# A linear-attention chain with two MLPs on one core: the order of the opening stretch, where weight words are converted, and the width of the preparation stretches

## The chip, the core and the metric

The kernel runs on one core of one Trainium2 chip. The metric is device time in microseconds (us), from one execution of the whole program; less is better. The engines are named as in the profile: PE is TensorE's matmuls, PEld its weight loads, DVE is VectorE, ACT ScalarE, POOL GpSimd, and SP (SyncE) issues most of the DMAs. L12 is line 12 of the kernel.

## The reference

Three stages feed one another. The first is a delta-rule attention over 4 x 8 batch-heads, 768 time steps and head width 48:

```python
k_n = k / (np.linalg.norm(k, axis=-1, keepdims=True) + 1e-06)
for t in range(S):
    kt, vt, bt = (k_n[:, :, t], v[:, :, t], beta[:, :, t, None])
    y[:, :, t] = np.einsum('bhd,bhde->bhe', q[:, :, t], state)
    v_old = np.einsum('bhde,bhd->bhe', state, kt)
    state = state + bt[:, :, :, None] * np.einsum('bhd,bhe->bhde', kt, vt - v_old)
```

Its output, 3072 tokens of width 384, goes through a first MLP, `h = x @ w_in`, a leaky relu with a slope per column, `g @ w_out` (inner width 2048), and then through a second one, `(silu(x @ w_gate) * (x @ w_val)) @ w_out` (inner width 1536). The weights arrive as 64-bit floats, the rest as 32-bit floats.

## The kernel before

**Attention.** Time is cut into 24 chunks of 32 steps. Within a chunk the recurrence becomes a triangular system for each batch-head, and what is needed is the inverse of a unit triangular 32 x 32 matrix. Four chunks make a window, so a window has 128 such matrices (4 chunks x 32 batch-heads), one to a partition. `pre_T` transposes k and q on PE, `pre_G` makes the products of k with k (part 0, tile `GL`) and of k with q (part 1, tile `mt`), and the inverse is then made by one of two generators that are advanced a step at a time:

- `lanes` eliminates row by row: 31 steps of a multiply (L252) and a subtract (L260), the first 10 columns on VectorE and the others on GpSimd; with loads and transposes 37 steps. It uses no PE. Windows 2 to 5 use it.
- `lanes2` eliminates only two 16 x 16 blocks (L321, L323) and gets the rest from two products on PE: the first (L337, `out1`) for 16 matrices of each partition group at a time, `z` = 0 for chunks 0 and 1 of the window and `z` = 1 for chunks 2 and 3, then the second (L360) and a subtract (L369). Windows 0 and 1 use it.

`do_KS`, `do_QS`, `do_U`, `do_S`, `do_Y` and `do_XT` are then the recurrence of one chunk: small PE products, with a subtract, copies or adds on VectorE and ScalarE after each.

**Conversion.** No engine here takes 64-bit floats, so each weight slice (128 x 384) is turned into 32-bit words: one ScalarE operation (L514), three VectorE operations (L522, L524, L528), and then a split into a rounded part and a remainder: L535 on ScalarE, L536 on VectorE for odd slices and on GpSimd for even ones. The generator `conv` (`all_w1`) does this for the first MLP's 32 slices, 97 steps in all, three steps to a slice; `go(conv, 3)` is one slice.

**MLPs.** The first MLP takes two chunks (256 tokens) at a time: a block n has 16 units j. A unit is `H1` (nine PE matmuls, L595), two relus on ScalarE (L605, L606), a combination on VectorE (L608, tile `pn`), a split on ScalarE and GpSimd (L612, L613), and two and a half units later `O1` (nine matmuls, L624). So there are 12 blocks, of which block 0 runs beside the conversion. The second MLP (L682, L711) follows.

**Order.** The order of all work is written out by hand. `prelude` is a straight list: loads, window 0, chunks 0 and 1, and 16 steps of conversion in between. After it everything hangs on a table of events, each at a time counted in units, one unit being one `H1`: `at(time, function)`. Sorted, this gives the order on every engine; an engine then runs its instructions in that order. `base(c)` is the unit at which chunk c's recurrence begins (20 and 25.7 for chunks 4 and 5, 8(c-2) for the others), so window w is prepared in the 32 units from P = base(4w) - 32. PE's time ahead of the table is called the opening below.

Matmuls in 32-bit floats show two records each in the trace, so 64 small matmuls of the program are 128 records. `warm` issues matmuls on a constant.

Of the kernel before, what the change touches and what calls it, by code (L numbers as in the profile page):

```python
# [24 lines left out]
def kernel(  # L25
# [25 lines left out]
    nc = tc.nc  # L51
# [133 lines left out]
    class Lanes:  # L185
# [19 lines left out]
        def turn_X(self, i):  # L205
            r = slice(i * HC, i * HC + HC)
            nc.vector.transpose(TT_t[self.w].rearrange("p y i -> p i y")[:, r], self.X[:, r])

        def norm(self):
            self.s, self.r, self.n, self.a = (self.new("sm" + z, "sm" + z, [128, C]) for z in "srna")  # L210
            ss = free_view(self.L, 0, [[C + 1, C]])
            s0, r, a = self.s, self.r, self.a
            nc.scalar.activation(out=s0, in_=ss, func=AF.Sqrt)
            nc.vector.tensor_scalar(r, s0, 2e-6, 1e-12, op0=ALU.mult, op1=ALU.add)
            nc.vector.tensor_tensor(r, r, ss, ALU.add)
            nc.vector.reciprocal(r, r)
            nc.vector.tensor_tensor(a, r, self.bl, ALU.mult)
            nc.vector.tensor_copy(free_view(self.X, 0, [[C + 1, C]]), a)
# [78 lines left out]
    def lanes2(w, early=False):  # L297
# [29 lines left out]
        nc.gpsimd.memset(Dm[:, :, HC:C], 0.0)  # L327
        TT_t[w] = t.new("TT", "TT", [128, 32, C], 2)
        t.turn_X(1)
        yield  # L330
        G, TT = GL.pop(w), TT_t[w]
        ps = [bank(early and z == 1, "pi") for z in range(2)]

        def out1(z):
            for y in range(HC * z, HC * z + HC):
                for b in range(4):
                    nc.tensor.matmul(  # L337
                        ps[z][rows(b), (y % HC) * HC:(y % HC) * HC + HC],
                        G[rows(b), y, :],
                        TT[rows(b), y, HC:C],  # L340
                        start=True,
                        stop=True,
                        skip_group_check=True,
                    )

        N = HC * HC
        uv = t.new("tmp", "tmp", [128, 512])
        out1(0)
        nc.scalar.activation(out=uv[:, 0:N], in_=ps[0][:, 0:N], func=AF.Copy)
        out1(1)  # L350
        nc.scalar.activation(out=uv[:, N:2 * N], in_=ps[1][:, 0:N], func=AF.Copy)
        nc.vector.transpose(Dm.rearrange("p y s -> p s y")[:, 0:HC], t.X.rearrange("p i j -> p j i")[:, 0:HC])
        yield
        t.turn_X(0)
        yield
        for z in range(2):
# [14 lines left out]
            )  # L371
            yield

    LANES2 = 4 + HC - 1 + 5

    def rows(b):
        return slice(32 * b, 32 * b + 32)
# [77 lines left out]
                nc.scalar.activation(out=sv, in_=sp[a][:, 0:DM], func=AF.Copy)  # L455

    def do_Y(c):
        m, U, yp = m_t.pop(c), U_t.pop(c), y_ps.pop(c)
        for h in range(H):
            for b in range(4):  # L460
                nc.tensor.matmul(
# [313 lines left out]
    def prelude():  # L775
# [28 lines left out]
        load_nat(1, "k", nat)  # L804
        nc.sync.dma_start(out=alpha_r, in_=moe_alpha.rearrange("(j p) -> j p", p=128))
        load_k2(0)
        load_w1(4, 5, 6, 7)
        load_beta(1)
        go(conv, 3)
        for c in range(4):  # L810
            pre_G(c, (0,), early=c % 2 == 1)
        go(conv, 3)
        inv = lanes2(0, True)
        go(inv, 2)
        n = 0
        for b1 in range(2):
            for half in range(2):
# [13 lines left out]
            for half in range(2):  # L831
                pre_T(1, "k", b1, half, nat)
        load_nat(1, "q", nat)
        load_w1(8, 9, 10, 11)
        warm(12)
        go(inv, C)
        do_QS(0)
        do_U(0)
        pre_G(2, (1,), early=True)
        go(conv, 2)  # L840
        do_S(0)
        load_k2(1)
# [9 lines left out]
        do_U(1)
        go(conv, 2)
        for z in range(2):
            pre_T(1, "q", 0, z, nat)
        do_S(1)
        load_k2(2)
        load_w1(*range(20, 2 * J1))
        do_Y(1)
        go(conv, 2)  # L860
        for z in range(2):
            pre_T(1, "q", 1, z, nat)
# [11 lines left out]
    for w in range(1, NWIN):  # L874
        P = base(4 * w) - 32
        if w == 1:
            for z in range(4):
                at(0.6 + z, pre_G, 4 + z)
            l0, l1, n = 5, 18, LANES2
        else:  # L880
            at(P - 5, load_nat, w, "k", nat)
            at(P - 1, load_beta, w)
            for z in range(4):
                at(P + 1.2 + z, pre_T, w, "k", z // 2, z % 2, nat)
            at(P + 5, load_nat, w, "q", nat)
# [12 lines left out]
        for z in range(n):
# [97 lines left out]
```

## Time and profile before

| | us |
|---|---|
| median of 3 runs (lowest, highest) | 1206.99 (1203.62, 1210.70) |
| the profiled execution: its own time | 1208.26 |
| its span, first to last instruction | 1206.5 |
| opening, span's start to the first `H1` | 77.65 |
| block 0 of the first MLP (first `H1` to the next block's) | 92.85 |
| block 1 | 58.9 |
| PE busy / VectorE busy over the span | 1102.4 (91%) / 612.2 (51%) |

The shares over the whole span hide the stages: from about 740 us on, the second MLP keeps PE busy without a break, and nothing that is changed here lies there. What there is to read is the opening and the first MLP's blocks, each from its own stretch. Blocks are told by the start of their first `H1`.

### The profile page before, as it was taken

The numbers are of one execution on the slowest core, as the hardware profiler recorded it, in microseconds if no ns is written. First come the engines' busy times: TensorE is split into PE (matmuls) and PEld (weight loads), VectorE is DVE, ScalarE is ACT, GpSimd is POOL, SyncE is SP. The second block draws the span as 40 slices with busy tenths as digits, with TensorE's granted clock in tenths as the row PEclk, the third lists the DMA queues.
The fourth block names the chain that finished last, engine by engine and source line by source line (L and its number), as shares of the span: only waits on it lengthen the run. The fifth ranks groups of instructions, "written<-read, shape, count | busy, mean of one in ns | idle before, by whom it ended". The sixth has DMA issues, their size and how long they took to land.

```text
span 1206.5 us, 38212 instructions
## 1 busy us (share of the span) xinstructions
PE 1102.4 (91%) x16657; PEld 1063.2 (88%) x16657; DVE 612.2 (51%) x1283; ACT 444.8 (37%) x1160; POOL 313.6 (26%) x476
## 2 busy tenths in 40 slices
PE   6567779989998998999899998999999999999996
PEld 6556679889987998899799988999999999999995
DVE  5369952396369439736954346333333333333332
ACT  3145434425533543454344465222222222222221
POOL 4024222164237326423732356100000000000000
PEclk8588869989999999999999999999999999999998
DMA  9282003233323423342233145010101010101000
GB/s 216 81 280 42 2 3 81 55 94 96 80 68 82 117 58 82 86 101 69 56 89 83 31 145 151 1 40 1 40 1 40 1 40 1 40 1 40 8 13 20
DMA packets 140084, 76.50 MB, mean 63 GB/s; under 512 B 104000, under 2 KB 134624, under 8 KB 139916
## 3 DMA queue, kind: packets, MB, share of 16 engines
q1 hardware_dynamic: 139340, 73.45, 22.4%
q8 instruction: 130, 2.13, 0.7%
q0 software_dynamic: 576, 0.61, 0.2%
q14 instruction: 38, 0.31, 0.1%
HBM read 57.52 MB, written 16.52 MB: 61 GB/s over the span
## 4 chain that ended last, share of the span: by engine, by line
PE 58%; DVE 15%; issue 10%; POOL 4%; ACT 3%; DMA 1%; SPq 0%; POOLq 0%; DVEq 0%; ACTq 0%
PE gv L682 21%; PE o L711 10%; PE o L624 10%; PE h L595 10%; DVE pn L608 3%; DVE X L260 2%; DVE tmp L252 2%; PE pg L167 1%; POOL gh L613 1%; PE pt L148 1%; PE pk L396 1%; PE pst L440 1%; DVE wf L528 1%; DVE we L522 1%; PE py L396 1%
## 5 line engine op out<-in xcount | busy, mean ns | idle before, releaser
L682 PE MATMUL gv<-x2s,w 128*128 128x384 f32 x1728 | 316.9, 335 | 0.0
L682 PEld LDWEIGHTS gv<-x2s,w 128*128 128x128 f32 x1728 | 303.3, 188 | 0.0
L624 PE MATMUL o<-gh,w 128*128 128x256 f32 x1728 | 261.1, 294 | 29.2 <-ACT gh L612 13.8
L595 PE MATMUL h<-xh,w 128*128 128x256 f32 x1152 | 247.3, 291 | 17.1 <-ACT pn L606 14.7
L624 PEld LDWEIGHTS o<-gh,w 128*128 128x128 f32 x1728 | 224.8, 194 | 42.7 <-POOL gh L613 16.6
L613 POOL TENSOR_TENSOR gh<-pn,gh 128x256 fp32r<-128x256 f32 x192 | 150.2, 782 | 374.2 <-ACT gh L612 310.2
L595 PEld LDWEIGHTS h<-xh,w 128*128 128x128 f32 x1152 | 198.4, 197 | 21.9 <-ACT pn L606 16.7
L608 DVE SCALAR_TENSOR_TENSOR pn<-pn,nalpha 128x256 f32<-128x256 f32 x192 | 100.8, 525 | 178.9 <-ACT pn L606 175.9
L595 PE MATMUL h<-xl,w 128*128 128x256 f32 x576 | 166.6, 289 | 3.2 <-DVE xl L487 2.6
L711 PE MATMUL o<-w,us 128*128 128x384 f32 x864 | 165.3, 336 | 0.0
L612 ACT ACTIVATE gh<-pn 128x256 fp32r<-128x256 f32 x192 | 80.2, 418 | 224.3 <-DVE pn L608 224.3
L711 PEld LDWEIGHTS o<-w,us 128*128 128x128 f32 x864 | 151.1, 188 | 0.0
L694 DVE TENSOR_TENSOR sg<-sg,gv 128x384 f32<-128x384 f32 x96 | 53.2, 554 | 174.3 <-ACT sg L692 174.2
L595 PEld LDWEIGHTS h<-xl,w 128*128 128x128 f32 x576 | 113.6, 197 | 3.7 <-DVE xl L487 3.7
L697 ACT ACTIVATE us<-u 128x384 fp32r<-128x384 f32 x96 | 50.5, 526 | 165.0 <-DVE u L695 165.0
L667 POOL TENSOR_TENSOR x2s<-x2r,x2s 128x384 fp32r<-128x384 f32 x24 | 24.2, 1036 | 333.8 <-ACT x2s L666 333.8
L692 ACT ACTIVATE sg<-gv 128x384 f32<-128x384 f32 x96 | 47.1, 491 | 168.8 <-PE gv L682 168.8
L605 ACT ACTIVATE pn<-h 128x256 f32<-128x256 f32 x192 | 72.4, 377 | 99.7 <-PE h L595 97.1
L698 DVE TENSOR_TENSOR us<-u,us 128x384 fp32r<-128x384 f32 x96 | 53.7, 559 | 62.8 <-ACT us L697 62.8
L695 DVE TENSOR_TENSOR u<-sg,gv 128x384 f32<-128x384 f32 x96 | 53.2, 554 | 45.8 <-PE gv L682 45.6
L606 ACT ACTIVATE pn<-h 128x256 f32<-128x256 f32 x192 | 72.8, 379 | 0.0
L536 POOL TENSOR_TENSOR w<-wf,w 128x384 fp32r<-128x384 f32 x34 | 38.4, 1130 | 72.0 <-ACT w L535 70.8
(102 smaller groups left out, 1068.9 us busy)
## 6 DMA issues: line engine op xcount, KB each, us to landing
w<-in_moe_w_out_dram SPq DMA_DIRECT2D x28, 384.0 KB
w2d<-wf SPq DMA_DIRECT2D x36, 192.0 KB
wf<-w2d SPq DMA_DIRECT2D x36, 192.0 KB
w<-in_moe_w_in_dram SPq DMA_DIRECT2D x16, 384.0 KB
nat<-in_k_dram SPq DMA_DIRECT2D x24, 192.0 KB
k<-in_k_dram SPq DMA_DIRECT2D x96, 48.0 KB
x2d<-xs SPq DMA_DIRECT2D x12, 384.0 KB
w<-in_moe_w_gate_dram SPq DMA_DIRECT2D x12, 384.0 KB
```

The source lines that it names most:

```text
L595: nc.tensor.matmul(ps[:, 0:N1], w[:, a, kk * 128:kk * 128 + 128], x[b][:, kk, :], start=(i == 0), stop=(i == 3 * NK - 1),)
L605: nc.scalar.activation(out=pn[:, 1], in_=hv, func=AF.Relu, scale=-1.0)
L606: nc.scalar.activation(out=pn[:, 0], in_=hv, func=AF.Relu)
L608: nc.vector.scalar_tensor_tensor(out=g, in0=pn[:, 1], scalar=nalpha[:, j:j + 1], in1=pn[:, 0], op0=ALU.mult, op1=ALU.add)
L612: nc.scalar.activation(out=gh[:, 0], in_=g, func=AF.Copy)
L613: nc.gpsimd.tensor_tensor(gh[:, 1], g, gh[:, 0], ALU.subtract)
L624: nc.tensor.matmul(o[:, dm // 2, (dm % 2) * N1:(dm % 2) * N1 + N1], w[:, a, dm * 128:dm * 128 + 128], g[:, b], start=(j == 0 and i == 0 an ...
L682: nc.tensor.matmul(p[:, 0:N2], w2[j, z][:, a, kk * 128:kk * 128 + 128], x[:, b, kk], start=(i == 0), stop=(i == 3 * NK - 1),)
L694: nc.vector.tensor_tensor(sg, sg, ps[0], ALU.mult)
L695: nc.vector.tensor_tensor(u, sg, ps[1], ALU.mult)
L698: nc.vector.tensor_tensor(us[:, 1], u, us[:, 0], ALU.subtract)
L711: nc.tensor.matmul(o2_t[n][t][:, 0:DM], us[:, a, t * 128:t * 128 + 128], w[:, b, :], start=(j == 0 and i == 0), stop=(j == J2 - 1 and i == 2),
```

## The change

Line numbers in the changed file are 4 to 5 higher from L208 on, and 12 higher at the end. Four things are changed.

1. `lanes2` for window 0 makes the product pair of chunks 0 and 1 complete first; the second half's first product is issued behind it, and its second product and subtract at the end of the opening. The opening is written in another order around it, with fewer `warm` matmuls (4 and 6 instead of 8 and 12), and the k-q products of chunks 2 and 3 (`pre_G(2, (1,))`, `pre_G(3, (1,))`) move from the opening to units 0.6 and 1.6.
2. 41 steps of `conv` instead of 16 are issued in the opening, and 56 instead of 81 in units -0.5 to 13.5. Two more weight slices are loaded ahead of the q loads of window 1, and six instead of four behind them.
3. Window 1 uses `lanes` (37 steps, units 6.6 to 18.5) instead of `lanes2` (24 steps, units 5 to 18).
4. Windows 2 to 5: `lanes` runs from P+15 to P+31.5 instead of P+17.3 to P+31; q's loads move from P+5 to P+4.5, its transposes from P+9.2 to P+7.2, and `pre_G` from P+13.2 to P+11.2.

```diff
         TT_t[w] = t.new("TT", "TT", [128, 32, C], 2)
         t.turn_X(1)
-        yield
         G, TT = GL.pop(w), TT_t[w]
-        ps = [bank(early and z == 1, "pi") for z in range(2)]
+        ps = [None, None]
 
         def out1(z):
+            ps[z] = bank(early, "pi")
...
-        out1(0)
-        nc.scalar.activation(out=uv[:, 0:N], in_=ps[0][:, 0:N], func=AF.Copy)
-        out1(1)
-        nc.scalar.activation(out=uv[:, N:2 * N], in_=ps[1][:, 0:N], func=AF.Copy)
-        nc.vector.transpose(Dm.rearrange("p y s -> p s y")[:, 0:HC], t.X.rearrange("p i j -> p j i")[:, 0:HC])
-        yield
-        t.turn_X(0)
+        t.turn_Dm(Dm)
         yield
         for z in range(2):
+            out1(z)
+            nc.scalar.activation(out=uv[:, z * N:z * N + N], in_=ps[z][:, 0:N], func=AF.Copy)
+            if z == 0:
+                t.turn_X(0)
+            yield
...
-        load_w1(4, 5, 6, 7)
+        load_w1(*range(4, 10))
...
-        load_w1(8, 9, 10, 11)
-        warm(12)
-        go(inv, C)
+        load_w1(*range(10, 16))
+        warm(6)
+        go(inv, LANES2 - 13 - 4)
+        go(inv)
+        go(conv, 4)
+        go(inv)
+        go(conv, 2)
         do_QS(0)
         do_U(0)
-        pre_G(2, (1,), early=True)
-        go(conv, 2)
+        go(conv, 3)
         do_S(0)
...
-    CONV_DONE, CONV_END = 16, 14.0
+    CONV_DONE, CONV_END = 41, 14.0
...
+            for z in range(2):
+                at(0.6 + z, pre_G, 2 + z, (1,))
             for z in range(4):
-                at(0.6 + z, pre_G, 4 + z)
-            l0, l1, n = 5, 18, LANES2
+                at(2.6 + z, pre_G, 4 + z)
+            l0, l1, n = 6.6, 18.5, LANES
...
-            l0, l1, n = P + 17.3, P + 31, LANES
+            l0, l1, n = P + 15, P + 31.5, LANES
...
-                box["g"] = lanes2(w) if w == 1 else lanes(w, 10)
+                box["g"] = lanes(w, 10)
```

What stands on PE in the opening, from the `warm` matmuls to the second chunk, before (`pi` is the bank of the two products, `pg` of `pre_G`, `pu`, `pst`, `py`, `pk` and `px` of the recurrence):

```order
L742 MATMUL warm<-ident 96x96 x12
L337 MATMUL pi<-TT,GL 32x16 x128
L360 MATMUL pi<-tmp,Dm 32x16 x128
L422 MATMUL pu<-v,TT 32x48 x32
L167 MATMUL pg<-kqt 32x32 x32
L440 MATMUL pst<-U,k_105 64x48 x32
L461 MATMUL py<-U,mt 32x48 x32
L396 MATMUL pk<-St,kqt 32x48 x32
L396 MATMUL py<-St,kqt 32x48 x32
L167 MATMUL pg<-kqt 32x32 x32
L483 MATMUL px<-ident,ys 128x128 x3
L422 MATMUL pu<-v,TT 32x48 x32
```

And now:

```order
L746 MATMUL warm<-ident 96x96 x6
L342 MATMUL pi<-TT,GL 32x16 x64
L364 MATMUL pi<-tmp,Dm 32x16 x64
L342 MATMUL pi<-TT,GL 32x16 x64
L426 MATMUL pu<-v,TT 32x48 x32
L444 MATMUL pst<-U,k_105 64x48 x32
L400 MATMUL pk<-St,kqt 32x48 x32
L465 MATMUL py<-U,mt 32x48 x32
L400 MATMUL py<-St,kqt 32x48 x32
L426 MATMUL pu<-v,TT 32x48 x32
L487 MATMUL px<-ident,ys 128x128 x3
L465 MATMUL py<-U,mt 32x48 x32
```

One second product of 64 has gone to the end of the opening, where it stands ahead of window 1's last transposes and the first `H1`, and two `pg` groups of 32 have left the opening.

What stands on VectorE behind the subtract that completes the inverse of chunks 0 and 1, up to the copy of the first state, before (two subtracts, since both halves are done there):

```order
L369 TENSOR_TENSOR TT<-TT,pi 128x16x16 x2
L180 TENSOR_TENSOR mt<-pg,mask 128x256
L522 TENSOR_SCALAR we<-wf 128x384
L524 SCALAR_TENSOR_TENSOR wf<-wf,we 128x384
L536 TENSOR_TENSOR w<-wf,w 128x384
L453 COPY St<-pst 128x384
```

And now:

```order
L373 TENSOR_TENSOR TT<-TT,pi 128x16x16
L526 TENSOR_SCALAR we<-wf 128x384
L528 SCALAR_TENSOR_TENSOR wf<-wf,we 128x384
L540 TENSOR_TENSOR w<-wf,w 128x384
L532 SCALAR_TENSOR_TENSOR wf<-w_109,wf 128x384
L526 TENSOR_SCALAR we<-wf 128x384
L528 SCALAR_TENSOR_TENSOR wf<-wf,we 128x384
L532 SCALAR_TENSOR_TENSOR wf<-w_110,wf 128x384
L526 TENSOR_SCALAR we<-wf 128x384
L528 SCALAR_TENSOR_TENSOR wf<-wf,we 128x384
L540 TENSOR_TENSOR w<-wf,w 128x384
L532 SCALAR_TENSOR_TENSOR wf<-w_111,wf 128x384
```

Three slices of conversion (eleven instructions) now stand between that subtract and the state copy, where three instructions stood. Down to the first `pn` there are 13, 13, 12 and 7 of L526, L528, L532 and L540.

What stands on VectorE between two `pn` in the second half of block 0, before:

```order
L608 SCALAR_TENSOR_TENSOR pn<-pn,nalpha 128x256
L524 SCALAR_TENSOR_TENSOR wf<-wf,we 128x384
L536 TENSOR_TENSOR w<-wf,w 128x384
L528 SCALAR_TENSOR_TENSOR wf<-w_133,wf 128x384
L522 TENSOR_SCALAR we<-wf 128x384
L321 TENSOR_TENSOR tmp<-L,X 128x126
L323 TENSOR_TENSOR X<-X,tmp 128x2x9x7
L524 SCALAR_TENSOR_TENSOR wf<-wf,we 128x384
L528 SCALAR_TENSOR_TENSOR wf<-w_134,wf 128x384
L522 TENSOR_SCALAR we<-wf 128x384
L321 TENSOR_TENSOR tmp<-L,X 128x128
L323 TENSOR_TENSOR X<-X,tmp 128x2x8x8
```

And now:

```order
L612 SCALAR_TENSOR_TENSOR pn<-pn,nalpha 128x256
L257 TENSOR_TENSOR tmp<-L,X 128x220
L265 TENSOR_TENSOR X<-X,tmp 128x22x10
L528 SCALAR_TENSOR_TENSOR wf<-wf,we 128x384
L257 TENSOR_TENSOR tmp<-L,X 128x210
L265 TENSOR_TENSOR X<-X,tmp 128x21x10
L532 SCALAR_TENSOR_TENSOR wf<-w_136,wf 128x384
L257 TENSOR_TENSOR tmp<-L,X 128x200
L265 TENSOR_TENSOR X<-X,tmp 128x20x10
L526 TENSOR_SCALAR we<-wf 128x384
L528 SCALAR_TENSOR_TENSOR wf<-wf,we 128x384
L540 TENSOR_TENSOR w<-wf,w 128x384
```

Fewer conversions and three larger elimination steps stand between two `pn`. From the first `pn` of block 0 to that of block 1, VectorE now has 17 of L526, 17 of L528, 18 of L532 and 9 of L540, the first 30 of the 37 steps of `lanes`, 16 `pn`, and 14 operations of the attention (2 subtracts, 4 state adds, 6 `mt`, 2 `xl`).

## Rows read from the trace of the kernel before

**Rows 1.** Busy us and instructions by engine, clock, DMA: blocks 0 and 1.

```profile
core 0: us, PE busy (x) PEld busy (x) DVE busy (x) ACT busy (x) POOL busy (x), PEclk, DMA share, GB/s
77.65:170.50 92.85, 66.45 (x1428) 59.95 (x1428) 82.19 (x170) 44.27 (x113) 31.90 (x34) 0.81 0.21 58
170.50:229.40 58.90, 58.33 (x1421) 55.24 (x1414) 17.96 (x37) 26.87 (x77) 14.10 (x19) 0.92 0.26 61
```

**Rows 2.** Sum and mean of the same view over blocks 2, 4, 6 and 8.

```profile
sum 220.40, PE 195.82 PEld 183.45 DVE 186.01 ACT 78.84 POOL 119.88; mean PE 48.95 PEld 45.86 DVE 46.50 ACT 19.71 POOL 29.97
```

**Rows 3.** Sum and mean of the same view over blocks 3, 5 and 7.

```profile
sum 156.20, PE 154.56 PEld 147.45 DVE 65.86 ACT 83.15 POOL 47.11; mean PE 51.52 PEld 49.15 DVE 21.95 ACT 27.72 POOL 15.70
```

**Rows 4.** PE in the opening by time: start, us, what, xcount [idle before <-releaser].

```profile
40.18 1.84 PE L337 MATMUL pi<-TT,GL 32*32 32x16 f32 x123 [4.44 <-issue]
...
43.74 1.90 PE L360 MATMUL pi<-tmp,Dm 16*32 16x16 f32 x128 [1.67 <-issue]
47.20 1.84 PE L360 MATMUL pi<-tmp,Dm 16*32 16x16 f32 x124 [1.56 <-issue]
...
66.59 0.27 PE L422 MATMUL pu<-v,TT 32*32 32x48 f32 x4 [3.17 <-issue]
...
77.65 0.38 PE L595 MATMUL h<-xh,w 128*128 128x256 f32 x1 [0.58 <-ACT xh L486]
```

**Rows 5.** Busy time and DMA rate in one stretch of 2 us.

```profile
36.00:38.00 2.00, 0.00 (x0) 0.00 (x0) 0.00 (x0) 0.12 (x1) 0.00 (x0) 0.50 0.87 325
```

**Rows 6.** VectorE in block 0 by line: xcount | busy us, mean ns | idle before.

```profile
L524 DVE SCALAR_TENSOR_TENSOR wf<-wf,we 128x384 int32<-128x384 int32 x27 | 18.1, 672 | 1.1
L528 DVE SCALAR_TENSOR_TENSOR wf<-w,wf 128x384 int32<-128x384 int32 x27 | 18.0, 666 | 0.4
L522 DVE TENSOR_SCALAR we<-wf 128x384 int32<-128x384 int32 x26 | 13.7, 527 | 0.0
L536 DVE TENSOR_TENSOR w<-wf,w 128x384 fp32r<-128x384 f32 x14 | 9.1, 650 | 2.4 <-ACT w L535 2.4
L608 DVE SCALAR_TENSOR_TENSOR pn<-pn,nalpha 128x256 f32<-128x256 f32 x16 | 7.6, 476 | 0.0
...
L451 DVE TENSOR_TENSOR St<-pst,St 128x384 f32<-128x384 f32 x4 | 2.0, 547 | 0.0
L180 DVE TENSOR_TENSOR mt<-pg,mask 128x256 f32<-128x256 f32 x4 | 1.7, 420 | 1.4 <-ACT GL L177 1.3
...
L226 DVE TENSOR_SCALAR sms<-sms 128x32 f32<-128x32 f32 x1 | 0.2, 169 | 0.0
```

**Rows 7.** VectorE by time at the end of block 0.

```profile
173.68 0.48 DVE L608 SCALAR_TENSOR_TENSOR pn<-pn,nalpha 128x256 f32<-128x256 f32 x1 [7.30 <-ACT pn L606]
```

**Rows 8.** VectorE by line from 346 to 396 us, one whole run of `lanes`.

```profile
L252 DVE TENSOR_TENSOR tmp<-L,X 128x60 f32<-128x60 f32 (+29 forms) x31 | 12.2, 393 | 0.2
...
L524 DVE SCALAR_TENSOR_TENSOR wf<-wf,we 128x384 int32<-128x384 int32 x4 | 2.7, 684 | 0.0
...
L226 DVE TENSOR_SCALAR sms<-sms 128x32 f32<-128x32 f32 x1 | 0.2, 166 | 0.0
```

**Rows 9.** GpSimd by line over the same stretch.

```profile
L252 POOL TENSOR_TENSOR tmg<-L,X 128x21 f32<-128x21 f32 (+10 forms) x21 | 8.6, 408 | 0.9
L260 POOL TENSOR_TENSOR X<-X,tmg 128x21 f32<-128x21 f32 (+10 forms) x21 | 7.8, 371 | 1.6
```

**Rows 10.** GpSimd by line in block 0.

```profile
L536 POOL TENSOR_TENSOR w<-wf,w 128x384 fp32r<-128x384 f32 x14 | 15.6, 1112 | 20.4 <-ACT w L535 20.1
L613 POOL TENSOR_TENSOR gh<-pn,gh 128x256 fp32r<-128x256 f32 x16 | 13.3, 830 | 49.3 <-issue 33.5 <-ACT gh L612 9.7 <-DMA w<-in_moe_w_in_dram 3.1
```

**Rows 11.** PE by time in block 4, its longest wait.

```profile
372.36 0.38 PE L624 MATMUL o<-gh,w 128*128 128x256 f32 x1 [2.82 <-ACT gh L612]
```

**Rows 12.** PE by time in block 1: the second products of window 1.

```profile
174.68 1.91 PE L360 MATMUL pi<-tmp,Dm 16*32 16x16 f32 x128
...
179.58 1.26 PE L360 MATMUL pi<-tmp,Dm 16*32 16x16 f32 x128
```

**Rows 13.** Block 3 by time: q's loads on SP, and its first transpose on PE.

```profile
298.32 3.79 SPq L100 DMA_DIRECT2D nat<-in_q_dram  x4
...
315.58 0.60 PE L148 MATMUL pt<-ident,nat 128*128 128x128 f32 x4
```

More of the change, by code (lines that the diff above doesn't have):

```diff
@@ L207, in turn_X, with turn_Dm @@
             nc.vector.transpose(TT_t[self.w].rearrange("p y i -> p i y")[:, r], self.X[:, r])
+        def turn_Dm(self, Dm):
+            nc.vector.transpose(
+                Dm.rearrange("p y s -> p s y")[:, 0:HC], self.X.rearrange("p i j -> p j i")[:, 0:HC]
+            )
         def norm(self):
@@ L372, in lanes2 @@
             yield
-    LANES2 = 4 + HC - 1 + 5
+    LANES2 = 4 + HC - 1 + 6
     def rows(b):
@@ L457, in do_Y @@
     def do_Y(c):
-        m, U, yp = m_t.pop(c), U_t.pop(c), y_ps.pop(c)
+        m, U, yp = m_t.pop(c), U_t[c], y_ps.pop(c)
         for h in range(H):
@@ L813, in prelude @@
         inv = lanes2(0, True)
-        go(inv, 2)
+        go(inv, 3)
         n = 0
@@ L843, in prelude @@
         load_v(2)
-        load_w1(*range(12, 20))
+        load_w1(*range(16, 24))
+        go(conv, 3)
+        do_KS(1)
+        go(conv, 3)
         do_Y(0)
-        do_KS(1)
-        go(conv, 2)
         do_QS(1)
-        pre_G(3, (1,), early=True)
+        do_U(1)
+        go(conv, 3)
         do_XT(0)
         go(conv, 2)
[L852 to L855, printed above, removed]
+        do_Y(1)
+        go(conv, 3)
         do_S(1)
         load_k2(2)
[L858 to L862, printed above, removed]
-        do_XT(1)
-        go(conv, 2)
+        load_w1(*range(24, 2 * J1))
+        go(conv, 3)
+        do_XT(1)
+        go(conv, 3)
+        go(inv)
+        go(conv, 3)
+        go(inv)
+        for z in range(4):
+            pre_T(1, "q", z // 2, z % 2, nat)
+        go(conv, 3)
     def base(c):
         return {4: 20, 5: 25.7}.get(c, 8 * (c - 2))
-    CONV_DONE, CONV_END = 16, 14.0
+    CONV_DONE, CONV_END = 41, 14.0
     CONV_N = 3 * 2 * J1 + 1 - CONV_DONE
@@ L884 @@
                 at(P + 1.2 + z, pre_T, w, "k", z // 2, z % 2, nat)
-            at(P + 5, load_nat, w, "q", nat)
+            at(P + 4.5, load_nat, w, "q", nat)
             for z in range(4):
-                at(P + 9.2 + z, pre_T, w, "q", z // 2, z % 2, nat)
+                at(P + 7.2 + z, pre_T, w, "q", z // 2, z % 2, nat)
             for z in range(4):
-                at(P + 13.2 + z, pre_G, 4 * w + z)
-            l0, l1, n = P + 17.3, P + 31, LANES
+                at(P + 11.2 + z, pre_G, 4 * w + z)
+            l0, l1, n = P + 15, P + 31.5, LANES
         box = {}
```

2 lines of the change are left out of this document (1 added, 1 removed).

## The prediction

> **What bounds the kernel now.** I read stretch by stretch, since the shares of the whole span mix stages with different limits. From about 740 us PE works without a break and nothing changed lies there, so the time has to come out of the opening, of blocks 0 and 1, and of the blocks that prepare a window.
>
> The windows of blocks 0 and 1 come first [rows 1]. In block 0 VectorE is busy 82.19 of 92.85 us while PE has 66.45, so VectorE is the bound and it idles 10.66 us. Of this, 7.30 lie at one place at the block's end: VectorE, whose next instruction is a `pn`, waits for ScalarE's relu, which follows an `H1` [rows 7]; ahead of that `H1` PE stands in `lanes2`'s products of window 1. Block 1 is the opposite: PE 58.33 of 58.90, VectorE 17.96, and a mean granted clock of 0.92 of 2.4 GHz, so it spent some of its time at 1.2 GHz.
>
> The later blocks alternate. The even ones, with `lanes` in them, last 220.40/4 = 55.1 us with PE busy 48.95, so PE idles 24.58 us over the four [rows 2]; their VectorE is busy 46.5. The odd ones last 156.20/3 = 52.07 with PE at 51.52 [rows 3]. In the even blocks, then, PE waits, and its longest wait in block 4 is an `O1` for `gh`, 2.82 us [rows 11]: a chain from VectorE's `pn` through ScalarE that stands in VectorE's queue behind elimination steps.
>
> The opening, by PE's order of time [rows 4], is a third kind. PE starts again at 40.18, 43.74 and 47.20, each time for 1.84 to 1.90 us of 123 to 128 records, after waits of 1.56 to 1.67 that the trace puts to nothing ("issue"). So a set of 128 records costs some 3.5 us whatever it computes, half of it waiting for instructions. The wait of 4.44 comes just behind a stretch in which the weight loads move 325 GB/s [rows 5].
>
> The skill's "Runtime: NRT & Kernel Launch", section "Instruction fetch mechanics", says that instructions come in blocks of 256 and that crossing a block is mostly hidden. The trace disagrees here: 128 matmul records with as many weight loads are followed by 1.6 us of waiting [rows 4]. By the page, removing 128 records would save only their some 1.9 us of execution.
>
> **The change part by part.** The sum is made against the profiled execution's own 1208.26 us (a span of 1206.5 and 1.8 around it); the median of the runs shown is 1.27 lower.
>
> *Opening, -0.7.* Two `pg` groups, 64 products or 128 records, leave: one period, 43.74 - 40.18 = 3.55 us less. `lanes2` has as many products as before. Two more weight slices (2 x 384 KB, 1.2 us each at 325 GB/s [rows 5]) go ahead of the q loads and prolong the burst in which the 4.44 wait lies: +2.4. The first `H1` waits 0.58 for the `xh` of chunk 1 [rows 4]; the half product now put between hides this and about as much again: -1.0. Along the recurrence some eight hand-offs from PE to VectorE or ScalarE and back now may find conversion in front. VectorE's load down to the first `pn`, at block 0's durations [rows 6], is 13 x .527 + 13 x .672 + 12 x .666 + 7 x .650 = 28.1 us, which fits into the 33.9 us from 43.74 to 77.65, but not loosely. I take two hand-offs that meet half a slice (some .75 us each): +1.5. Together -0.65. Bounds: all eight meeting a whole slice's VectorE operations (about 1.9) would be +15; at the other end `H1` comes 9 earlier, if supply waits go with the burst (4.44 and 3.17) beside the removed period, less the 2.4.
>
> *Block 0, -10.4.* VectorE is the bound, so I count its work from the first `pn` to the next block's. Conversion, 17 x .527 + 17 x .672 + 18 x .666 + 9 x .650 = 38.2; 16 `pn`, 7.6; 14 attention operations, 8 x .547 + 6 x .420 = 6.9 [rows 6]. A whole `lanes` costs VectorE 34.2, the sum of the 17 groups in which its lines show from 346 to 396 us [rows 8]. Of its 37 steps 30 fall here, 27.7 by count; the last ones are the shortest, so I take 30 (bounds 27.7 and 34.2). Sum 82.7. Block 0's 27 groups add up to 91.4 where the busy union is 82.19, since neighbours overlap: a factor of .90, hence 74.4. For idle time I take 8, between 10.66 - 7.30 = 3.4 (the one wait gone, with the products that made it) and 55.1 - 46.5 = 8.6 (even blocks). Block 0 is then 82.4, not 92.85. The two `pg` groups that arrive cost PE at most 3.55, hidden while PE has 66.45; if that cover goes they are on the path. L524 takes 684 ns beside `lanes` against 672 without [rows 6, 8], so no surcharge on conversion. Bounds: -17 (27.7 for `lanes`, 3.4 idle: 72.4 + 3.4) and +3 (34.2, no overlap factor, 8.6 idle: 86.9 + 8.6).
>
> *Block 1, -4.6.* The second products of window 1 on PE, 1.91 + 1.26 [rows 12], vanish: -3.2. What the clock cost is .08 x 58.9 = 4.7; with a block 0 in which PE idles less, I give back a third, -1.4. `lanes`' last seven steps, some 4 us, hide under VectorE's 41 us of idle time. Bounds -3.2 and -7.9.
>
> *Blocks 2, 4, 6, 8, -12.3.* `lanes` spread over 16.5 units instead of 13.7. What elimination adds to VectorE is the even less the odd blocks' busy time, 46.50 - 21.95 = 24.55: over 13.7 units 1.79 us each, beside 21.95/16 = 1.37 of other work [rows 2, 3]. So in the stretch VectorE has 3.16 per unit against PE's 48.95/16 = 3.06: slightly over. After: 24.55/16.5 + 1.37 = 2.86, under PE. A small change turns the inequality, but waits from order stay, so I take half of the 24.58 PE idle. Bounds 0 and -24.6. q's loads move half a unit earlier and its transposes two, so the transposes come 1.5 units or some 4.9 us nearer to their loads. Before, the four loads ran from 298.32 for 3.79 us and the first transpose came at 315.58 [rows 13]: of the 13.5 us between, 8.6 are left, and the move costs nothing. GpSimd's part, 16.4 [rows 9], has more room, too.
>
> Sum: -0.7 - 10.4 - 4.6 - 12.3 = -28.0, so 1180.3 on the profiled time and **1179** on the median.
>
> **The rivals.** *A, the opening is held up.* VectorE and ScalarE take their queues in order, and three slices of conversion now stand between the completed inverse and the first state's copy. If six of eight hand-offs meet a slice's 1.9 us, `H1` comes 10 us later than forecast: 1189. For it: 28.1 us in 33.9. Against: PE's own supply takes 3.5 us per 128 records, in which VectorE gets through more than a slice.
>
> *B, the wider stretch gives nothing.* PE's waits in the even blocks are waits for order (`pn` behind any elimination step, then `gh` [rows 11]) and not load; then they last 16.5 units at a lower price each, and -12.3 falls away: 1191. For it: 46.5 of 55.1 is no full VectorE.
>
> *C, everything loosens.* The even blocks lose all idle time (-12.3 more) and the burst's waits vanish from the opening (-3.3 more): 1163.
>
> *D, slower: VectorE and GpSimd exclude each other in block 0.* Into the block that VectorE bounds come 16.4 us of `lanes` on GpSimd [rows 9], beside 13.3 of `gh` and nine conversions of 1.112, 10.0 [rows 10]. If none of these 39.7 us runs beside VectorE, block 0 is 74.4 + 39.7 + 8 = 122.1, +29.3 instead of -10.4: 1219. It decides from 28 of the 39.7 us on. Against: in the even blocks VectorE's 46.5 and GpSimd's 30.0 lie within 55.1 us [rows 2], so at least 21.4 overlap as recorded, though a blocked instruction may count as busy.
>
> In the skill, "SBUF — State Buffer", section "Who interferes with whom", says that a VectorE instruction with two inputs in SBUF and a GpSimd one that reads SBUF lock each other out for the whole instruction. By that rule D would hold for most pairs here; L524's 684 against 672 [rows 6, 8] does not show it.
>
> **How the numbers follow.** Forecast .52 (its own range 1169 to 1189), A .16, B .14, C .09, D .09. The likeliest gives 1179. The range leaves out D and the far half of C, and reaches from 1162 to 1202, where A and B together (1201) end. A difference of 0.5%, 6 us, is about what can be told from none (the runs spread over 7), so "same" is 1201 to 1213. Faster .86: the forecast, A and B but for .05 in which they fall together, and C; same .09: that .05 and half of D where the lock-out is partial; slower .05.
>
> **What would show it.** Right: the first `H1` at about 77 us; block 0 near 82 with VectorE busy near 74 and no single wait of 7 us; no `lanes2` products in block 1 and its length near 54; even blocks near 52 with shorter waits of PE for `gh`. Wrong: the first `H1` after 85, with VectorE or ScalarE named before PE's starts (A); even blocks still at 55 (B) or at 49 (C); GpSimd and VectorE instructions of block 0 longer than 1112, 830 and 672 ns, and the block over 93 (D). The forecast as a whole fails if the opening grows by as much as block 0 shrinks, because conversion has then only moved from one bound stretch to another.

## The result and the profile after

The changed kernel takes 1177.82 us (median of 4 runs, 1175.76 to 1178.39), the kernel before 1206.28 (4 runs): a ratio of 0.9757, 95% interval 0.9725 to 0.9789. The forecast was 1179 within 1162 to 1202. The profiled execution took 1177.41 us against 1208.26, 30.85 less. The sum came out, in part by luck: the terms of the stretches are off by 2.5 to 7.5 us each, in both directions.

| | before | after | change | forecast |
|---|---|---|---|---|
| opening, to the first `H1` | 77.65 | 69.41 | -8.2 | -0.7 |
| block 0 | 92.85 | 85.0 | -7.9 | -10.4 |
| block 1 | 58.9 | 58.6 | -0.3 | -4.6 |
| blocks 2, 4, 6, 8 | 220.4 | 199.0 | -21.4 | -12.3 |
| blocks 3, 5, 7 | 156.2 | 162.3 | +6.1 | 0 |
| all behind | | | +0.8 | 0 |

Blocks 0 and 1 by windows, after (columns as in [rows 1]: stretch, length, then busy us of PE, PEld, DVE, ACT, POOL, granted clock, DMA share, GB/s):

```profile
69.42:154.41 84.99, 64.15 (x1304) 58.01 (x1301) 72.34 (x152) 37.40 (x100) 42.41 (x66) 0.78 0.18 46
154.41:213.00 58.59, 56.28 (x1222) 53.01 (x1222) 26.57 (x64) 27.50 (x81) 16.61 (x26) 0.95 0.28 66
```

VectorE has 72.34 us in block 0 (forecast 74.4), but idles 12.65, not 8. In block 1 PE is busy 2.05 us less (forecast 4.6, of products and of clock), and yet the block is no shorter: PE now idles 2.31 us in it, 1.97 of them at its end, where the first `H1` of block 2 waits for the attention's output `xh`. Sum and mean of the even blocks 2 to 8 and, in the second fence, of the odd ones 3 to 7, against [rows 2] and [rows 3]:

```profile
sum 199.00, PE 183.68 PEld 173.63 DVE 179.40 ACT 79.62 POOL 119.76; mean PE 45.92 PEld 43.41 DVE 44.85 ACT 19.90 POOL 29.94
```

```profile
sum 162.30, PE 158.39 PEld 150.60 DVE 70.47 ACT 82.55 POOL 46.53; mean PE 52.80 PEld 50.20 DVE 23.49 ACT 27.52 POOL 15.51
```

PE's idle time in the even blocks fell from 24.6 to 15.3 us, and its busy time by 12.1: the last of a window's four `pre_G` groups, which stood in them, has moved into the odd block before (for window 2, into block 1), and the granted clock in them rose, from 0.97 to 1.00 in block 4. The odd blocks got 1.28 us of PE work each, and 0.75 of idle time.

PE in the opening by time, after (columns as in [rows 4]):

```profile
31.78 1.90 PE L342 MATMUL pi<-TT,GL 32*32 32x16 f32 x128 [6.08 <-DVE TT L207]
34.23 0.50 PE L364 MATMUL pi<-tmp,Dm 16*32 16x16 f32 x21 [0.55 <-issue]
35.30 1.62 PE L364 MATMUL pi<-tmp,Dm 16*32 16x16 f32 x106 [0.56 <-issue]
...
41.49 1.62 PE L342 MATMUL pi<-TT,GL 32*32 32x16 f32 x106 [4.29 <-issue]
...
45.60 1.17 PE L426 MATMUL pu<-v,TT 32*32 32x48 f32 x43 [2.02 <-issue]
...
69.41 0.37 PE L599 MATMUL h<-xh,w 128*128 128x256 f32 x1
```

The 4.29 us wait beside the weight loads is the 4.44 of [rows 4], no longer for the two more slices (in the nine kernels with PE's order as changed and 16 or 41 conversion steps it is 3.75 to 5.39, in the mean 4.4); the first `H1` waits for nothing; and the first product of the inverse starts at 31.78, where it started at 33.78. From that start to the first `H1`, PE's waits without a named releaser ("issue") add up to 9.9 us, and to 16.2 before; those for VectorE or ScalarE to 3.3, and 1.4 before. So the opening's gain lies mostly in the waits that the trace puts to nothing.

What VectorE waited for in block 0, after (engine, waiting line, releaser: us in all, times, longest):

```profile
DVE mt L180 <- ACT GL L177: 4.6, 4, 2.9
DVE w L540 <- ACT w L539: 3.3, 4, 1.9
DVE pn L612 <- ACT pn L610: 1.4, 2, 1.0
...
```

The wait of 7.30 for a `pn` [rows 7] is gone. The largest is now `mt`: its multiply stands in VectorE's queue for products that PE has not yet made, and everything else on VectorE stands behind it.

How VectorE sets the end of block 0 shows on ScalarE and PE there, by time:

```profile
153.56 0.42 ACT L616 ACTIVATE gh<-pn 128x256 fp32r<-128x256 f32 x1 [3.87 <-DVE pn L612]
153.88 0.47 ACT L490 ACTIVATE xh<-px 128x384 fp32r<-128x384 f32 x1
154.40 0.58 PE L599 MATMUL h<-xh,w 128*128 128x256 f32 x1 [2.73 <-ACT xh L490]
```

ScalarE waits 3.87 us for a `pn`, which VectorE makes behind elimination steps; the copy of `xh` stands behind that in ScalarE's queue, and block 1's first `H1` waits for `xh`.

### The profile page after: what moved, and what is told of

It reads as the page before. It is cut to its first block, busy times and chain, and to the rows that moved or that the text cites. A ratio compares the mean times of both kernels' runs of the same rounds, so it can differ in the third digit from the quotient of the medians.

```text
span 1175.7 us, 37218 instructions
## 1 busy us (share of the span) xinstructions
PE 1087.1 (92%) x16125; PEld 1049.6 (89%) x16125; DVE 621.9 (53%) x1313; ACT 444.4 (38%) x1158; POOL 330.4 (28%) x517
## 4 chain that ended last, share of the span: by engine, by line
PE 60%; DVE 19%; issue 13%; ACT 3%; POOL 2%; DMA 1%; POOLq 0%; DVEq 0%; SPq 0%; ACTq 0%
PE gv L686 21%; PE o L715 10%; PE o L628 10%; PE h L599 10%; DVE tmp L257 4%; DVE pn L612 3%; DVE X L265 2%; PE pg L167 2%; DVE wf L532 1%; PE pt L148 1%; PE pst L444 1%; PE py L465 1%; DVE wf L528 1%; PE pk L400 1%; POOL w L540 1%
## 5 line engine op out<-in xcount | busy, mean ns | idle before, releaser
L628 PE MATMUL o<-gh,w 128*128 128x256 f32 x1728 | 258.2, 293 | 22.8 <-POOL gh L617 9.6
L599 PE MATMUL h<-xh,w 128*128 128x256 f32 x1152 | 243.6, 288 | 12.7 <-ACT pn L610 6.7
L628 PEld LDWEIGHTS o<-gh,w 128*128 128x128 f32 x1728 | 223.1, 193 | 35.6 <-POOL gh L617 13.7
L599 PEld LDWEIGHTS h<-xh,w 128*128 128x128 f32 x1152 | 195.8, 194 | 15.7 <-ACT pn L610 7.3
L698 DVE TENSOR_TENSOR sg<-sg,gv 128x384 f32<-128x384 f32 x96 | 53.2, 554 | 175.9 <-ACT sg L696 175.9
L702 DVE TENSOR_TENSOR us<-u,us 128x384 fp32r<-128x384 f32 x96 | 53.7, 559 | 62.8 <-ACT us L701 62.8
L699 DVE TENSOR_TENSOR u<-sg,gv 128x384 f32<-128x384 f32 x96 | 53.2, 554 | 45.7 <-PE gv L686 45.5
L257 DVE TENSOR_TENSOR tmp<-L,X 128x31 f32<-128x31 f32 (+29 forms) x155 | 65.7, 424 | 1.4
```

Of the source, the lines that this page charges most:

```text
L257: eng.tensor_tensor(w, t.L[:, i + 1:C, i:i + 1].to_broadcast([128, n, m]), t.X[:, i:i + 1, c0:c0 + m].to_broadcast([128, n, m]), ALU.mult,)
L599: nc.tensor.matmul(ps[:, 0:N1], w[:, a, kk * 128:kk * 128 + 128], x[b][:, kk, :], start=(i == 0), stop=(i == 3 * NK - 1),)
L628: nc.tensor.matmul(o[:, dm // 2, (dm % 2) * N1:(dm % 2) * N1 + N1], w[:, a, dm * 128:dm * 128 + 128], g[:, b], start=(j == 0 and i == 0 an ...
L698: nc.vector.tensor_tensor(sg, sg, ps[0], ALU.mult)
L702: nc.vector.tensor_tensor(us[:, 1], u, us[:, 0], ALU.subtract)
```

## The experiments

Twelve kernels, each timed in three rounds beside the kernel before. "First `H1`" and the lengths are from each one's profiled execution. "As changed" is the changed kernel.

| | us | ratio, interval | first `H1` | block 0 | block 1 | blocks 4, 6, 8, mean |
|---|---|---|---|---|---|---|
| as changed | 1177.8 | 0.976 (.973, .979) | 69.4 | 85.0 | 58.6 | 49.1 |
| 16 conversion steps | 1194.7 | 0.989 (.987, .992) | 71.8 | 98.0 | 58.5 | 49.0 |
| products back | 1180.9 | 0.978 (.976, .981) | 74.8 | 81.2 | 58.1 | 49.1 |
| `lanes2` for window 1 | 1178.1 | 0.976 (.974, .978) | 72.0 | 71.3 | 70.0 | 49.0 |
| before, part 4 alone | 1195.4 | 0.990 (.987, .993) | 77.6 | 93.2 | 61.3 | 49.0 |
| narrow | 1191.3 | 0.985 (.983, .987) | 72.0 | 83.1 | 57.2 | 53.2 |
| early and narrow | 1187.7 | 0.982 (.980, .984) | 73.3 | 82.2 | 58.4 | 52.0 |
| column 24, window 1 | 1178.5 | 0.974 (.973, .976) | 71.5 | 80.5 | 62.8 | 49.1 |
| 47 conversion steps | 1175.9 | 0.973 (.970, .975) | 74.7 | 79.5 | 58.1 | 49.0 |
| halves together | 1179.8 | 0.977 (.974, .980) | 74.9 | 81.2 | 58.4 | 49.1 |
| 18 units | 1168.6 | 0.967 (.962, .971) | 68.8 | 82.5 | 57.9 | 47.0 |
| column 7 | 1186.8 | 0.983 (.979, .986) | 70.7 | 82.3 | 58.4 | 50.8 |
| 18 units, column 16, chunks 4 and 5 earlier | 1157.8 | 0.958 (.956, .961) | 70.1 | 84.1 | 57.0 | 45.6 |

**16 conversion steps.** Some of the `go(conv, n)` of the opening are cut or left out:

```diff
-    CONV_DONE, CONV_END = 41, 14.0
+    CONV_DONE, CONV_END = 16, 14.0
```

> The changed kernel with only 16 steps of conversion in the opening, as before, and 81 in units -0.5 to 13.5; all else as changed. Theory: VectorE bounds block 0 and has room in the opening, so the 25 steps cost nothing there and their price comes back in block 0. The first H1 stays at 69.4 us (within 1); block 0 grows by 25/3 slices x 2.14 us of VectorE x .90 = 16 us, from 85.0 to about 101; time about 1194 us. Rival: the conversions hold up the recurrence in the opening. Then the first H1 comes by 65 us or earlier and the time is at most 1190. Second rival: block 0 is bound by the waits between engines and not by VectorE's load; then it grows by under 8 us.

It took 16.9 us more than as changed. The first `H1` came no earlier, and in block 0 VectorE was busy 85.18 us:

```profile
71.75:169.71 97.96, 68.98 (x1303) 61.28 (x1301) 85.18 (x176) 44.90 (x114) 46.26 (x69) 0.76 0.15 38
```

So the 25 steps are free in the opening and cost their VectorE time in block 0. Both rivals fall.

**Products back.** The k-q products of chunks 2 and 3, 128 records, stand in the opening again:

```diff
         do_U(0)
+        pre_G(2, (1,), early=True)
...
         do_U(1)
+        pre_G(3, (1,), early=True)
...
-            for z in range(2):
-                at(0.6 + z, pre_G, 2 + z, (1,))
```

> The changed kernel with the k-q products of chunks 2 and 3 back in the opening (128 records on PE), as before. Theory of the prediction: the opening is bound by the supply of PE's instructions, some 3.5 us for 128 records whatever they compute, so the first H1 comes 3.5 us later, at 73.0; block 0 gets 1 to 2 us shorter, because VectorE no longer waits for these products there; time 1179 to 1180. Rival: only their execution counts (2 x 1.1 us), the first H1 at 71.6. Second rival: PE waits for VectorE and ScalarE along the recurrence and the products hide there; the first H1 stays at 69.4 to 70.

From the first product of the inverse to the first `H1` it took 42.4 us (32.45 to 74.82). In the nine kernels of the table with PE's order as changed and 16 or 41 conversion steps it took 36.3 to 39.9, in the mean 38.5. That is 2.4 to 6.0 more, 3.9 against the mean, where the products execute for 2 x 1.08. The waits without a named releaser add up to 12.5 us, against 8.5 to 11.9 in the nine; those for VectorE or ScalarE did not grow (1.2, against 1.8 to 4.4). So the supply price of one period, 3.55, fits better than the execution alone; with one profile each and such a spread, its size is not settled. Block 0 gave most of it back (81.2): it ends at 156.0, where the seven kernels with the changed opening and `lanes` end it between 151.3 and 155.5.

**`lanes2` for window 1.**

```diff
-                box["g"] = lanes(w, 10)
+                box["g"] = lanes2(w) if w == 1 else lanes(w, 10)
```

> The changed kernel with the inverse of window 1 made again from two 16 x 16 blocks and two products on PE, in units 6.6 to 18.5. Theory of the prediction: VectorE has some 7 us less in block 0, but waits some 7 us at its end behind PE's products, so block 0 stays at 83 to 87 us; block 1 gets 3.2 us of products, 58.6 to about 62; time 1181 to 1184. Rival: the full elimination costs block 0 what it saves in block 1, and block 0 falls to 80 or less; time 1174 to 1178.

My theory fell, and the rival is right. Block 0 became 13.7 us shorter and block 1 11.4 longer; the time is the same:

```profile
71.98:143.23 71.25, 57.54 (x1302) 52.76 (x1301) 60.30 (x137) 36.83 (x98) 26.08 (x28) 0.88 0.21 52
143.23:213.25 70.02, 67.29 (x1734) 63.10 (x1734) 24.15 (x48) 28.69 (x83) 16.09 (x23) 0.85 0.24 56
```

Against the fence of the kernel as changed, VectorE has 12 us less in the block that it bounds, and PE 11 us and 512 records more in the block that PE bounds, at a granted clock of 0.85 instead of 0.95. The third part of the change moves cost from one bound to the other, and beside the other three parts it is worth nothing.

**Before, part 4 alone.** The four edits of times P+... in the kernel before.

> The kernel before with only the fourth part of the change (elimination of windows 2 to 5 over 16.5 units instead of 13.7, q loads, q transposes and k-products earlier). Theory: that part alone gives what the traces show in blocks 2 to 8, even blocks together -21, odd ones +6, and block 1 gets one of window 2's product groups, +1.3: time about 1192 (14 less than before). Rival: the even blocks profit from the earlier parts too; then this gives less than 8 us.

It gave 13.1 us, with even blocks as in the changed kernel. So their gain needs nothing of the other parts, as the theory had it.

**Narrow; early and narrow.**

```diff
-            l0, l1, n = P + 15, P + 31.5, LANES
+            l0, l1, n = P + 17.3, P + 31, LANES
```

> The changed kernel with the elimination of windows 2 to 5 back in units P+17.3 to P+31 (13.7 units), while q's loads, transposes and the k-products stay early. Theory of the prediction: what counts is VectorE's load per unit, which goes back over PE's; the even blocks lose some 4 us each of what they gained (their idle time and clock), the odd ones give back under 1 each: time about 1190. Rival: the gain comes from the products moved out of the even blocks; then the time stays at 1178 to 1181.

> The changed kernel with the elimination of windows 2 to 5 in units P+15 to P+28.7: it starts as early as in the change, but is as dense as before (13.7 units). Theory of the prediction (density): the even blocks lose as much as with the narrow stretch at the old place, time 1187 to 1191. Rival: what counts is that the inverse is ready earlier, or that less of it lies in an even block's last units; then no loss, time at most 1180.

The second has P + 15, P + 28.7. They lose 13.5 and 9.9 us against as changed. So density counts most; the earlier start is worth some 3.6. Where it acts is seen in the narrow kernel's block 4, VectorE by time, between two `pn`:

```profile
347.03 0.62 DVE L257 TENSOR_TENSOR tmp<-L,X 128x220 f32<-128x220 f32 x1
347.69 0.48 DVE L265 TENSOR_TENSOR X<-X,tmp 128x220 f32<-128x220 f32 x1
348.09 0.78 DVE L532 SCALAR_TENSOR_TENSOR wf<-w,wf 128x384 int32<-128x384 int32 x1
348.79 1.00 DVE L257 TENSOR_TENSOR tmp<-L,X 128x210 f32<-128x210 f32 x1
349.82 0.46 DVE L265 TENSOR_TENSOR X<-X,tmp 128x210 f32<-128x210 f32 x1
350.21 0.64 DVE L612 SCALAR_TENSOR_TENSOR pn<-pn,nalpha 128x256 f32<-128x256 f32 x1
```

and PE there:

```profile
351.35 0.38 PE L628 MATMUL o<-gh,w 128*128 128x256 f32 x1 [2.82 <-ACT gh L616]
```

VectorE has no gap, `pn` comes when the queue ahead of it is done, and PE waits 2.82 us for what hangs on it: the wait of [rows 11] is back.

**18 units.** P + 15 to P + 33.

> The changed kernel with the elimination of windows 2 to 5 spread over 18 units, P+15 to P+33. Theory: in the thick part of the elimination VectorE still has no gap, so the even blocks gain another 1 to 1.5 us each, the odd ones lose 0.5; time 1173 to 1175. Rival: VectorE's load per unit is already under PE's (2.86 against 2.84 to 3.06), so the even blocks stay, the odd blocks get elimination into their full first units, and the time is 1178 or more.

It took 9.2 us less than as changed; the even blocks went to 47.0, PE's idle time in blocks 4, 6 and 8 from 10.9 to 6.7 us. That is better than both readings. The rival took the average load per unit for the load in the thick part.

**Column 7, and column 24 for window 1.** `lanes(w, 7)` for windows 2 to 5; `lanes(w, 24)` for window 1.

> The changed kernel with windows 2 to 5 eliminated up to column 7 instead of 10 on VectorE, the rest on GpSimd. VectorE loses 829 of 3685 elements a partition in either operation, about 1.6 us for a window; GpSimd has room (30 of 49 us). Theory (VectorE's queue holds up PE in the thick part): the even blocks gain about 1 us each, time 1173 to 1175. Rival (the engines hinder each other, or GpSimd's longer steps and its part of the split come late): the even blocks stay at 49 or grow, time 1178 or more.

> The changed kernel with window 1 eliminated up to column 24 instead of 10 on VectorE, so that GpSimd has hardly any of it. GpSimd loses about 16 us of work in block 0, VectorE gets some 1770 elements a partition in either of two operations, about 3.4 us by the slope of its own rows (0.20 us at 31 elements, 0.39 at 220). Theory of the prediction (the two engines run beside each other): block 0 grows by 2 to 3 us to 88, time about 1180. Rival D in part (they block each other): VectorE's instructions of 1.0 to 1.35 us, usually 0.56, become rare, block 0 falls by 5 us or more to 80, time 1173 or less.

Column 7 made things worse by 9 us. Sum and mean of blocks 4, 6 and 8, first as changed, then with column 7:

```profile
sum 147.20, PE 136.35 PEld 129.03 DVE 135.70 ACT 59.99 POOL 90.93; mean PE 45.45 PEld 43.01 DVE 45.23 ACT 20.00 POOL 30.31
```

```profile
sum 152.40, PE 138.94 PEld 130.70 DVE 141.41 ACT 59.56 POOL 107.81; mean PE 46.31 PEld 43.57 DVE 47.14 ACT 19.85 POOL 35.94
```

VectorE was given fewer elements and was busy longer, 47.14 for 45.23. Neither engine's work is free beside the other's. With column 24 the rival came nearly true in block 0, and not in the time. GpSimd is busy 30.4 us there instead of 42.4; VectorE, which was given more elements, is busy 68.7 instead of 72.3, with L532 at 614 ns instead of 706, and the block takes 80.5 us. But block 1 grew to 62.8, since PE idles 4.9 us in it: blocks 0 and 1 together take 143.4 us against 140.3 to 143.6 in kernels with column 10, and the time is the same.

**47 conversion steps.** `go(conv, 8)` for `go(conv, 2)` ahead of `do_QS(0)`.

> The changed kernel with 47 steps of conversion in the opening, the six more of them where VectorE waits from 41.6 to 48.2 us (between the inverse of chunks 0 and 1 and the first U). Theory: they hide there; block 0 loses 2 slices x 2.14 us x .90 = 3.9, time 1174. Rival: the first U's copy stands behind them on ScalarE and the weights for them are not yet there; the first H1 comes 3 us or more later and the time stays at 1177 or more.

The ratio cannot be told from that of the kernel as changed. The first `H1` came at 74.7, as the rival said. VectorE has 4.0 us less in block 0, as the theory said (3.9), and the block is 5.5 shorter; it ends at 154.2, as before the edit. Six more steps at this place win nothing.

**Halves together.** Both halves of window 0's products ahead of the recurrence:

```diff
         go(conv, 4)
-        go(inv)
+        go(inv, 3)
         go(conv, 2)
...
-        go(inv)
-        go(conv, 3)
-        go(inv)
+        go(conv, 3)
```

> The changed kernel with both halves of window 0's products ahead of the recurrence again (the second half's second product, 128 records, is not put off to the end of the opening); nothing else differs. Theory, after the runs so far: PE's opening is as long as its records are many, and the end of block 0 is set by VectorE, so the order of the halves hardly counts; the first U's product starts 3.5 us later, at 46 to 49 us, but the first H1 stays at 69 to 73 as in the kernels with the changed opening, block 0 ends at 154 to 156, time 1177 to 1180. Rival: putting the half off is what shortened the opening; the first H1 comes at 75 or later and the time is 1182 or more.

The first `H1` came at 74.9, later than in all eight kernels with the changed opening (68.8 to 73.3), so the rival is right on the opening. The theory is right on the end: block 0 ends at 156.1 and the time is 1179.8, not told apart from 1177.8. In the opening PE now waits for the recurrence ahead of the last products, where the half that was put off used to stand:

```profile
65.53 0.55 PE L487 MATMUL px<-ident,ys 128*128 128x128 f32 x3 [1.33 <-ACT ys L474]
67.61 1.12 PE L148 MATMUL pt<-ident,nat 128*128 128x128 f32 x8 [1.53 <-DVE St L455]
70.34 1.12 PE L148 MATMUL pt<-ident,nat 128*128 128x128 f32 x4 [1.60 <-DVE xl L491]
74.13 1.11 PE L148 MATMUL pt<-ident,nat 128*128 128x128 f32 x4 [2.67 <-ACT kqt L153]
```

PE's waits for VectorE or ScalarE in this stretch add up to 9.6 us, against 1.8 to 4.4 in the nine kernels with the half put off.

**18 units, column 16, chunks 4 and 5 earlier.**

```diff
-        return {4: 20, 5: 25.7}.get(c, 8 * (c - 2))
+        return {4: 18.5, 5: 24.5}.get(c, 8 * (c - 2))
...
-            l0, l1, n = P + 15, P + 31.5, LANES
+            l0, l1, n = P + 15, P + 33, LANES
...
-                box["g"] = lanes(w, 10)
+                box["g"] = lanes(w, 10 if w == 1 else 16)
```

> The kernel with the elimination over 18 units (P+15 to P+33), and with two more edits: windows 2 to 5 are eliminated up to column 16 on VectorE (GpSimd then has 680 of its 1771 elements a partition in either operation, and 15 steps instead of 21), and chunks 4 and 5 begin at units 18.5 and 24.5 instead of 20 and 25.7. Two readings. First, blocks 4, 6 and 8, against 47.1, 47.1 and 46.8 us: theory, the engines hinder each other (as up to column 7, where VectorE had fewer elements and took longer), so VectorE's added 2.1 us by elements come back as shorter waits, and the blocks stay within 0.3 us or fall by up to 1; rival, no hindrance, the blocks grow by 1 us each. Second, the starts of blocks 1 and 2, which wait 2 to 2.7 us for the attention's output: block 2 starts 1 to 2 us earlier against block 1's start (theory), or the wait only moves (rival: no change). Time 1164 to 1168 by the theories, 1171 or more by the rivals.

1157.8 us, 0.958 of before, and better than both theories. Sum and mean of blocks 4, 6 and 8, with 18 units alone and then with all three:

```profile
sum 141.00, PE 134.32 PEld 128.68 DVE 133.06 ACT 61.50 POOL 91.91; mean PE 44.77 PEld 42.89 DVE 44.35 ACT 20.50 POOL 30.64
```

```profile
sum 136.80, PE 132.79 PEld 128.00 DVE 127.82 ACT 60.15 POOL 72.89; mean PE 44.26 PEld 42.67 DVE 42.61 ACT 20.05 POOL 24.30
```

VectorE has 1091 elements a partition more in either operation of the elimination and is busy 1.7 us less; GpSimd 6.3 less. The blocks fall by 1.4 us each; the two chunks that begin earlier lie in block 1, so I put this down to column 16. Block 2's first `H1` no longer waits for `xh` and `xl` (1.98 and 1.87 us with 18 units alone), and the block is 45.7 us long instead of 50.9.

## Why the prediction was right, step by step

The misses were, for the opening -7.5, for block 0 +2.5, for block 1 +4.3, for the preparation blocks -3.0 and +0.8 behind them: together -2.9 on a forecast of -28.0. That they cancel is luck. What was foreseen with its mechanism is VectorE's load in block 0 and the gain of the wider stretch.

**Opening.** Of the four terms one fits: the two `pg` groups, taken at a period of 3.55, measured 2.4 to 6.0, in the mean 3.9. The Trainium skill's "Runtime: NRT & Kernel Launch", section "Instruction fetch mechanics", calls the crossing from one block of instructions to the next mostly hidden; an estimate by it would be the execution alone, 2.2 by the rows, just below that range, and the mean lies nearer to [rows 4]. The +2.4 for two more weight slices was wrong: they prolong no wait of PE. The +1.5 for hand-offs was wrong: with 25 steps fewer the first `H1` was no earlier. So rival A had no ground at 41 steps; with six more at one place the first `H1` did come later (74.7, after 42.0 us of the same stretch). The -1.0 for the half that is put off was too small: with the halves together the same stretch, 32.65 to 74.90, is 42.3 us long, 2.3 to 5.9 more than in the nine kernels. I had priced only the wait ahead of the first `H1`, not the other waits at the end of the recurrence that the products fill. What I had not costed is that the first product of the inverse starts earlier, by 2.0 us in this run and 0.4 to 2.2 in the kernels with the same order. A step of `lanes2` moved ahead of the transposes and fewer `warm` records could each do that; they were not tried apart, and why the waits without a named releaser fell by 6.3 us stays open beyond the two groups.

**Block 0.** The mechanism is shown: VectorE's load sets its end. In all fourteen profiles the block is 8.5 to 12.8 us longer than VectorE is busy in it, while that busy time goes from 60.3 (`lanes2` for window 1) to 85.2 us (16 steps) and the length from 71.3 to 98.0. The load was sized well, and not by luck. By the forecast's own count, from the first `pn` of block 0 (74.43) to that of block 1 (158.95), conversion is 38.2 (forecast 38.2), `pn` 7.8 (7.6), the attention 6.9 (6.9) and `lanes` 29.0 (30); VectorE's busy time is 73.6 (74.4). The idle time of 8 was too small, by 2.9 in that count, since new waits, above all 4.6 us for `mt`, took the place of the 7.30.

The ten kernels with 41 or 47 steps in the opening, the changed order of it or one edit back, and `lanes` for window 1 reach the first `H1` anywhere from 68.8 to 74.9 and end block 0 between 151.3 and 156.1; the three latest openings have blocks of 79.5 to 81.2. So time won in the opening is partly lost again in block 0: over the eight of them with 41 steps and column 10 for window 1, the end moves by some 0.6 us for each us of the first `H1` (an estimate, a line through their traces). By it some 4 of the opening's unforeseen 7.5 us lasted.

**Block 1.** The products left, but four `pg` groups of window 2 stand here instead of three (256 records for 192), and PE idles 1.7 us more, most of it ahead of block 2. I had moved `pre_G` in the sum for nothing; it crosses a block's border, and each odd block pays 1.28 us of PE for it.

**Preparation blocks.** Density is shown to be the cause in the main (narrow, early and narrow, 18 units). The half that I took for the idle time was a guess; 9.3 of 24.6 us went, and the odd blocks took 2.3 back. Of the -15.3 of even and odd blocks together, then, 7.0 are idle time and 8.3 PE's busy time: some 1.1 of it went to block 1 with its fourth product group, and the remainder, 7.2, is near what the clock gives, granted 0.03 higher over 220 us of even blocks (6.6, an estimate). [Rows 2] show the clock only mixed into busy time, and I had no term for it. Rival B falls. By the sign that I gave for C, even blocks at 49, it came true (49.75 in the mean); but 15.3 us of idle time stay, where C has none, and more than half of what these blocks lost is PE's busy time. So C falls in its size, though 18 units and column 16 show that it was the nearer one.

**D.** Its mechanism is there, its price never decided. I had dismissed it because L524 takes 684 ns beside `lanes` and 672 without [rows 6, 8]. Both rows were taken beside GpSimd's work. The same operation in the opening, where GpSimd is busy 4.4 of 24.4 us, by line from 45 to 69.4 us:

```profile
L528 DVE SCALAR_TENSOR_TENSOR wf<-wf,we 128x384 int32<-128x384 int32 x8 | 4.5, 558 | 0.6
```

and in block 0, after:

```profile
L532 DVE SCALAR_TENSOR_TENSOR wf<-w,wf 128x384 int32<-128x384 int32 x20 | 14.1, 706 | 0.2
L528 DVE SCALAR_TENSOR_TENSOR wf<-wf,we 128x384 int32<-128x384 int32 x19 | 13.0, 684 | 0.4
```

In that stretch of the opening seven of nine L532 take 0.55 to 0.56 us. The two others take 1.40 (from 50.88) and 1.03 (from 66.78), and exactly there GpSimd works, from 50.87 and from 66.24. Over the whole execution the 34 L528 and 25 L532 that have no GpSimd instruction beside them take 505 to 564 ns, in the mean 552 and 551; the 34 and 43 others up to 1245 and 1398, in the mean 661 and 778. Against 552 and 551, hindrance costs some 5.6 us of block 0 in these 39 instructions (an estimate from the means).

The kernel before pays it as well: 672 and 666 ns [rows 6] are means of hindered and unhindered instructions, and 45 L524 and 34 L528 of that trace without GpSimd beside them take 553 and 551. That is why no surcharge on conversion was needed, though the comparison that I gave for it shows nothing.

The Trainium skill's "SBUF — State Buffer", section "Who interferes with whom", says that such a pair locks each other out. The runs with columns 7, 16 and 24 agree in direction. That each pair does so for the whole instruction no run here shows: 44 of the 77 instructions beside GpSimd take 600 ns or less.

By parts, undone or done alone: the conversion steps 16.9 us, the wider stretch 13.1, the products 3.1 and putting off a half 2.0 (neither told from nothing: the intervals of the ratios overlap that of the kernel as changed), `lanes` for window 1 0.2 (nothing). They add up to more than 28.5; opening and block 0 share one end, so that parts undone singly need not add up.

## What to carry to other kernels

Work that one engine must do goes where another bounds the time, and two adjacent stretches whose end is set by one engine's queue belong together: of time won in the first, a part is lost again in the second. Spread filler work on the engine that others wait for by its thickest stretch, not by its mean load. Before calling an instruction unhindered, compare its duration with a stretch in which the suspected neighbour is idle.

## What was not expected of the hardware

Kernels with the same PE order in the opening reach the first `H1` between 68.8 and 73.3 us. The waits without a named releaser move: at the same place 4.29 us as changed, 3.75 with 18 units, and 5.39 with `lanes2` for window 1. One and the same VectorE instruction takes 0.55 us, and 1.40 where a GpSimd instruction had just begun. And giving VectorE 1091 elements more of GpSimd's work in each operation made VectorE's own busy time 1.7 us a block shorter.
